# An attention loop whose SyncE transfers wait for earlier ones, so that 1.2 MB at most is under way

## The chip, the cores and the metric

The kernel runs on one core of a Trainium2 chip. The metric is the device time of one execution in microseconds. The times shown are those of three executions and of one that was profiled.

## The reference, cut to what matters

Attention over 8 batches of 8 heads (576 positions, 64 wide), four heads with a local mask and four with a strided one, then a mixture of 8 experts with one expert a token and a skip test.

```python
scores = scale * np.matmul(q, k.transpose(0, 1, 3, 2))
mask_local = (rel >= 0) & (rel < stride)
mask_strided = (rel >= 0) & (pos[None, :] % stride == pos[:, None] % stride)
scores = np.where(masks[None], scores, -1000000000.0)
attn = np.exp(scores - np.max(scores, axis=-1, keepdims=True))
attn = attn / (np.sum(attn, axis=-1, keepdims=True) + 1e-09)
x = np.matmul(attn, v)                 # then to 4608 tokens of 512
...
do_compute = x @ w_skip > 0
e_idx = np.argmax(xc @ w_gate, axis=1)
h = np.maximum(xc[mask] @ w1[e], 0.0)
y[mask] = gate_w[mask, None] * (h @ w2[e])
out[do_compute] = xc + y
```

## The kernel before

The attention works in 32 units: for each of 8 batches two units of the local heads (kind 0) and two of the strided ones (kind 1). The loop at the end of `attn_moe` runs over them. In its pass n TensorE (PE) multiplies queries and keys of unit n + 2 (`qk`, line 198), turns the scores of unit n (`tex`, line 233), multiplies with the values of unit n - 1 (`pv`, line 267) and turns the outcome of unit n - 2 (`xpose`, line 309). VectorE (DVE) adds masks and takes maxima (lines 205 to 211), divides (lines 275 to 282) and routes the tokens; GpSimd (POOL) subtracts the maxima (line 213); ScalarE (ACT) takes the exponential (line 241) and copies (line 311). The order on PE, DVE and POOL is written out by hand in the loop; that on ACT and SyncE is left to the planner, which keeps SyncE's transfers in the order of the program.

All plain transfers are issued by SyncE, one after the other:
- `loadq` and `loadk` (lines 172 and 177), one half of a batch's queries or keys in two transfers of 288 to 304 KB. They are issued in the odd passes, for the half batch n // 2 + 3.
- `loadv` (line 184), three transfers of 390 KB for kind 0 and two for kind 1, in the even passes, for the next batch.
- `store` (lines 290 and 295), the rows of a half batch that was done some units before: two transfers of 288 KB for kind 0, and six of 90 to 99 KB for kind 1.
- `wdma` (line 567), weights of the first expert, 512 KB each, five of them in the loop's last passes.

The tiles set how far loads run ahead: six for queries and keys together, two for the values of each kind, three for raw weights. A transfer that would write a tile waits until the last reader of the tile is done. Each transfer also counts up one of eight semaphores in turn when it lands, and the next one on that semaphore waits for it: so at most eight are under way, whatever their size.

Before the loop stand the loads of the first batch and half of the second. Behind it come the last stores, the routing of the last batch, and then the experts, whose tokens POOL gathers from the output by indirect DMA and whose weights SyncE loads two ahead of their use.

Of the kernel before, what the change touches and what calls it, by code (L numbers as in the profile page):

```python
# [2 lines left out]

# [19 lines left out]
NA = S // ST  # L23
HP = 64
# [14 lines left out]
QL = (S, S + PAD)  # L39
VL = (3, 2)  # L40
BIG = -(2.0 ** 33)
ESTR = 5120
COUNTED = {4: 3, 7: 5}
PB = 3
# [30 lines left out]
def make_consts():  # L75
# [8 lines left out]
    for t in range(5):  # L84
        ml[:, t] = np.where((i + 1 <= w) & (w <= i + ST) & (w >= (ST if t == 0 else 0)), 0.0, BIG)
    w = np.arange(SQ)[None, :]
    ms = np.where((i // NA == w // NA) & (w % NA <= i % NA) | (i >= SQ), 0.0, BIG)
    put("ml", ml.reshape(128, -1))
# [17 lines left out]
def attn_moe(ctx: ExitStack, tc: tile.TileContext, q, k, v, w9d, w1d, w2d, cst, out, NB=B):  # L106
    nc = tc.nc
# [5 lines left out]

    table = dpool.tile([NE * ESTR, 4], I32, name="table")

# [36 lines left out]
    frame = [ap.tile([128, 2, 6, HP], F32, name=f"frame{i}") for i in range(2)]  # L152

    qt_, kt_, vt_ = {}, {}, {}

    def part(d, L, kind, name):
        t = zp.tile([128, 2, S + PAD], F32, name=f"{name}{kind}", tag="qk", bufs=6)[:, :, 0:L[kind]]
# [11 lines left out]
    def loadq(b, kind):  # L169
        t, d = qtile(b, kind)  # L170
        for j in range(2):
            nc.sync.dma_start(t[:, j], d[:, j])

    def loadk(b, kind):
        t, d = ktile(b, kind)
        for j in range(2):
            nc.sync.dma_start(t[:, j], d[:, j])

    def loadv(b, kind):
        n, m = (LB, SP)[kind], VL[kind]  # L180
        vt_[b, kind] = vt = ap.tile([128, n, 4, 65], F32, name=f"vt{kind}", tag=f"vt{kind}", bufs=2)
        vr = vt.rearrange("p (t n) h c -> p t (n h c)", t=m)
        for t in range(m):
            nc.sync.dma_start(vr[:, t], v[b][kind * VL[0] + t])

# [96 lines left out]
    def store(b, kind):  # L284
        ob = out[b * S:(b + 1) * S, kind * 256:kind * 256 + 256]
        x = xt_[b, kind]
        for i in range(2):
            oc = ob[:, i * 128:(i + 1) * 128]
            if kind == 0:
                nc.sync.dma_start(oc.rearrange("(n q) c -> q n c", q=HP), x[HP * i:HP * i + HP])  # L290
            else:
                orr = oc.rearrange("(a r) c -> a r c", r=ST)
                for r in range(3):
                    m = (ST - r + 2) // 3
                    nc.sync.dma_start(orr[:, r::3, :], x[HP * i + r * NA:HP * i + (r + 1) * NA, 0:m, :])


    xT_ = {}
# [18 lines left out]
    def tiles(g):  # L317
        return GT
# [91 lines left out]
            counted(of)  # L410

    stores = []
    SYNC = mybir.DependencyInfo(mybir.DependencyClass.Sync, mybir.DependencyReason.DATA)

    def behind(i, them):
        for x in them:
            tc.add_manual_dep(i, x.name, SYNC, reason="the rows of a batch are stored before they are taken")
# [20 lines left out]
    def mul(g):  # L438
        o = slice(GOFF[g], GOFF[g + 1])
        lo, eh = hot_[g]  # L440
        pm = ap.tile([128, GT, NP, 24], BF16, name="hpm", tag="hpm", bufs=2)
        G.tensor_tensor(pm, eh.unsqueeze(2).broadcast_to([128, GT, NP, 24]),
                        parts[:, o, :].unsqueeze(3).broadcast_to([128, GT, NP, 24]), op=ALU.mult)
        hot_[g] = lo, pm
# [45 lines left out]
    def pick(b):  # L490
# [6 lines left out]
        V.tensor_reduce(fsel[:, 0:1], t1, axis=AX.X, op=ALU.add)  # L497
        V.tensor_scalar(fsel[:, 1:2], fsel[:, 0:1], float(ESTR), None, op0=ALU.mult)
        V.tensor_copy(isel[:, 0:2], fsel[:, 0:2])
# [15 lines left out]
    def sort(b):  # L515
# [10 lines left out]
        def places():  # L526
# [5 lines left out]
            V.tensor_reduce(orf[:, 0, :], big, axis=AX.X, op=ALU.add)  # L532
            V.tensor_scalar(orf[:, 1, :], orf[:, 0, :], float(ESTR), None, op0=ALU.mult)
            V.tensor_copy(order, orf)
# [28 lines left out]
    def wdma(key, e, j0, j1, after=()):  # L563
        for j in range(j0, j1):
            raw = early.tile([128, 1024], F32, name="raw", tag="raw", bufs=3)
            src = (w1d if j < 4 else w2d)[bass.ds(e, 1), j % 4]
            i = nc.sync.dma_start(raw, src.rearrange("o p c -> (o p) c")).ins
            for x in after:
                tc.add_manual_dep(i, x.name, SYNC, reason="the tokens come first")
            raw_[key, j] = raw  # L570
# [231 lines left out]
    p = ps("T")  # L802
# [10 lines left out]
    a, z = qtile(0, 0), ktile(0, 0)  # L813
# [27 lines left out]
    plan[CB + 1] = (None, 4 * CB + 11, None, None)  # L841
    pool_order = ExitStack()
    pool_order.enter_context(tc.manual_schedule(engines={G.engine, T.engine, V.engine}))
    for n, (b, pr) in enumerate(units):

        if pr % 2 == 0:
            if b + 1 < NB:
                loadv(b + 1, pr // 2)
            if n == 8:
                spare = tvw[:, CMAX:CE[0] * CE[1] + CT, :].rearrange("e (a n) c -> a e (n c)", n=NE)  # L850
                nc.sync.dma_start(spare, fill.rearrange("p n c -> p (n c)")[0:spare.shape[0]].unsqueeze(1)
                                  .broadcast_to([spare.shape[0], NE, 4 * NE]))
        else:
            if n > 4:
                store(units[n - 4][0], units[n - 4][1] // 2)
            g = n // 2 + 3
            if g // 2 < NB:
                loadq(g // 2, g % 2)
                loadk(g // 2, g % 2)
        if n + LA >= len(units) and "h" not in pool:  # L860
            zctx.close()
            pool["h"] = ctx.enter_context(tc.tile_pool(name="hpool", bufs=1, side="right", reuse_waits="tile"))
        g = [i for i, x in enumerate(GROUPS) if x[1] == b]

        front = [qk(*units[n + LA])] if n + LA < len(units) else []
        if n > 0:
            front.append(pv(*units[n - 1]))
        seq = [tex(b, pr)]
        if g and pr == 2:
            seq = [xpose(*units[n - 2])] + seq  # L870
        for x in front[:-1]:
            next(x)

        if len(front) > 1:
            run(seq.pop(0))
        if late:
            next(late[0])
        next(front[-1])
        put = [place(x) for x, it in plan.items() if it[3] == n]
        full = n == plan[CB][3]  # L880
        rank = []
        if ranked is not None:
            rank = [route2(ranked, of=COUNTED.get(b - 1))]
            for _ in range(tiles(ranked) + 1):
                next(rank[0])
            ranked = None

        if b > CB:
            run(*late)
            late = []  # L890
        for x in front:
            next(x, 0)
        run(*rank, *late, *front)
        if full:
            run(*put)
            tabled()
        late = []
        if b > 0 and pr == 2:
            seq = [score(b - 1, 0), score(b - 1, 1)] + seq
        if n > 1 and not (g and pr == 2):  # L900
            seq.append(xpose(*units[n - 2]))
        run(*seq)
        if not full:
            run(*put)
        if g and pr == 3:
            norm(g[0])
        if g and pr == 2:
            late = [route1(g[0])]
        if g and pr == 3:
            if b > CB:  # L910
                run(route2(g[0], of=COUNTED.get(b)))
            else:
                ranked = g[0]
        if b == PB + 2 and pr == 0:
            pick(PB)
        if (b, pr) in RESTS:
            j = RESTS.index((b, pr))
            wrest("e", j, j + 1)
        if (b, pr) in CASTS:
            j = CASTS.index((b, pr))  # L920
            wcast("e", j, j + 1)
        if b == CB + 2 and pr == 3:
            count(CB)
        if n == 1:
            G.tensor_copy(parts[:, :, 0:2], con["pk"].rearrange("p (t c) -> p t c", c=2))
        for x, it in plan.items():
            for f, at in zip((hot, gates, mul), (it[1], it[0], it[2])):
                if at == n:
                    f(x)
        if b == PB + 2 and pr == 3:  # L930
            e0 = nc.sync.value_load(isel[0:1, 0:1], min_val=0, max_val=NE - 1)
            wdma("e", e0, 0, 1)
        if b == PB + 2 and pr == 1:
            s0 = G.value_load(isel[0:1, 0:1], min_val=0, max_val=NE - 1)
        if (b, pr) in FETCH:
            j = FETCH.index((b, pr)) + 1
            wdma("e", e0, j, j + 1)
        if b == CB + 2 and pr == 1:
            rows("e", s0, *CE, eng=G)
            gather("e", "e", "e", last=(CB + 1) * S)  # L940
    pool_order.close()
    nr = len(GROUPS) - 1
    gates(CB + 1)
    mul(CB + 1)
    engines = ExitStack()
    engines.enter_context(tc.manual_schedule(engines={T.engine, A.engine, V.engine, G.engine}))
    run(pv(*units[-1]), xpose(*units[-2]), xturn("e"), xpose(*units[-1]))
# [7 lines left out]
    psum, bufs = pctx.enter_context(tc.tile_pool(name="psumT", bufs=1, space=PSUM, reuse_waits="tile")), {"S": 2, "T": 3, "PV": 2, "R": 1}  # L955
    s0n = G.value_load(isel[0:1, 2:3], min_val=0, max_val=(NE - 1) * ESTR + CE[0] * CE[1])
    ga = ffn1a("e")
# [201 lines left out]
```

## Time and profile before

| | us |
|---|---|
| three executions | 448.38, 450.92, 454.01 |
| their median | 450.92 |
| the profiled execution | 451.93 |
| its span, first to last instruction | 450.2 |
| PE busy | 412.2 |
| DVE busy | 280.2 |
| ACT busy | 186.6 |
| POOL busy | 142.6 |

The mean clock that was granted to PE in the profiled execution is 0.975 of full speed. Three executions lie within 5.6 us of each other, so that a single one says little about a difference of that size. SyncE moved 79.19 MB by its queue (q1 in the profile), POOL 10.37 MB by its own (q0), and 0.82 MB were instructions (q8 and q14).

In the rows of the profile an engine's name with a q is its sequencer: "SPq L172 ... x2" are two transfers issued at line 172. The time beside such a row is that of issuing, not of moving the bytes. "[1.30 <-X]" behind a row says that the engine stood idle for 1.30 us ahead of it and what ended that.

### The profile page before, as it was taken

The numbers are of one execution on the slowest core, as the hardware profiler recorded it, in microseconds if no ns is written. First come the engines' busy times: TensorE is split into PE (matmuls) and PEld (weight loads), VectorE is DVE, ScalarE is ACT, GpSimd is POOL, SyncE is SP. The second block draws the span as 40 slices with busy tenths as digits, with TensorE's granted clock in tenths as the row PEclk, the third lists the DMA queues.
The fourth block names the chain that finished last, engine by engine and source line by source line (L and its number), as shares of the span: only waits on it lengthen the run. The fifth ranks groups of instructions, "written<-read, shape, count | busy, mean of one in ns | idle before, by whom it ended". The sixth has DMA issues, their size and how long they took to land.

```text
span 450.2 us, 12195 instructions
## 1 busy us (share of the span) xinstructions
PE 412.2 (92%) x4991; PEld 370.6 (82%) x4992; DVE 280.2 (62%) x606; ACT 186.6 (41%) x370; POOL 142.6 (32%) x200
## 2 busy tenths in 40 slices
PE   6989898999789767999899999999999999999994
PEld 3766777777676655889799799999999999999984
DVE  4565695989997776781476464464474564755610
ACT  1334353536255416632533343444544535544400
POOL 3334444443555355024023318014024022200201
PEclk8899996999999889999999999999999999999998
DMA  8999987979995135515257476456566565645101
GB/s 296 397 393 322 369 283 270 296 239 321 309 378 164 34 101 154 179 62 146 86 162 229 131 226 209 140 166 206 163 200 184 161 210 181 218 150 183 48 20 42
DMA packets 51805, 90.38 MB, mean 201 GB/s; under 512 B 8251, under 2 KB 27963, under 8 KB 51745
## 3 DMA queue, kind: packets, MB, share of 16 engines
q1 hardware_dynamic: 45249, 79.19, 52.8%
q0 software_dynamic: 6496, 10.37, 8.0%
q8 instruction: 40, 0.66, 0.6%
q14 instruction: 20, 0.16, 0.1%
HBM read 75.16 MB, written 14.91 MB: 200 GB/s over the span
## 4 chain that ended last, share of the span: by engine, by line
PE 50%; DMA 1%; POOL 0%; DVE 0%; POOLq 0%; issue 0%
PE S L648 15%; PE S L650 15%; PE S L649 15%; PE PV L740 2%; PE T L642 1%; DMA xg<-out_dram,tab 1%; PE PV L782 0%; PE PV L780 0%; PE PV L781 0%; PE S L756 0%; PE S L755 0%; PE S L757 0%; POOL out_dram L728 0%; PE T L767 0%; PE S L642 0%; PE PV L642 0%
## 5 line engine op out<-in xcount | busy, mean ns | idle before, releaser
L648 PE MATMUL S<-xh,w1h 128*128 128x342 f32 (+6 forms) x248 | 78.6, 317 | 0.2 <-DVE hl L661 0.2
L650 PE MATMUL S<-xh,w1l 128*128 128x342 f32 (+6 forms) x248 | 76.7, 309 | 0.0
L649 PE MATMUL S<-xl,w1h 128*128 128x342 f32 (+6 forms) x248 | 76.5, 309 | 0.0
L728 POOL DMA_INDIRECT out_dram<-ot,tab x25 | 28.0, 1120 | 152.1 <-DVE ot L726 143.6
L648 PE MATMUL S<-hh,w2h 128*128 128x288 f32 (+5 forms) x192 | 59.5, 310 | 0.5 <-DVE hl L661 0.5
L650 PE MATMUL S<-hh,w2l 128*128 128x288 f32 (+5 forms) x192 | 58.0, 302 | 0.0
L649 PE MATMUL S<-hl,w2h 128*128 128x288 f32 (+5 forms) x192 | 57.9, 302 | 0.0
L660 ACT ACTIVATE hh<-S 128x342 fp32r<-128x342 f32 (+6 forms) x64 | 28.0, 437 | 63.4 <-PE S L650 58.3
L584 DVE TENSOR_TENSOR w1l<-raw,w1h 128x1024 fp32r<-128x1024 f32 x32 | 39.0, 1223 | 20.0 <-ACT w1h L578 20.0
L648 PEld LDWEIGHTS S<-xh,w1h 128*128 128x128 f32 x248 | 46.9, 189 | 0.9 <-issue 0.4
L649 PEld LDWEIGHTS S<-xl,w1h 128*128 128x128 f32 x248 | 46.8, 189 | 0.1
L213 POOL TENSOR_TENSOR sm<-sm,mx 128x480 f32<-128x480 f32 (+1 forms) x32 | 28.5, 910 | 57.7 <-DVE mx L211 36.7
L650 PEld LDWEIGHTS S<-xh,w1l 128*128 128x128 f32 x248 | 46.7, 188 | 0.0
L198 PE MATMUL S<-kt,qt 64*64 64x54 f32 (+1 forms) x1280 | 34.4, 244 | 13.4 <-issue 5.0
L584 DVE TENSOR_TENSOR w2l<-raw,w2h 128x1024 fp32r<-128x1024 f32 x32 | 39.1, 1223 | 9.8 <-ACT w2h L578 9.6
L198 PEld LDWEIGHTS S<-kt,qt 64*64 64x64 f32 x1280 | 28.1, 142 | 20.6 <-issue 8.5
L620 POOL DMA_INDIRECT xg<-out_dram,tab x25 | 33.9, 1357 | 33.9 <-issue 13.6
L661 DVE SCALAR_TENSOR_TENSOR hl<-S,hh 128x342 fp32r<-128x342 f32 (+6 forms) x64 | 30.9, 483 | 17.8 <-ACT hh L660 17.7
L311 ACT COPY xT<-T 128x512 f32<-128x512 f32 (+4 forms) x56 | 22.2, 441 | 36.8 <-PE T L309 36.6
L648 PEld LDWEIGHTS S<-hh,w2h 128*128 128x128 f32 x192 | 36.1, 188 | 0.8 <-DVE hl L661 0.8
L645 DVE TENSOR_TENSOR xl<-T,xh 128x288 fp32r<-128x288 f32 (+7 forms) x30 | 13.1, 468 | 37.3 <-ACT xh L644 37.3
L649 PEld LDWEIGHTS S<-hl,w2h 128*128 128x128 f32 x192 | 36.3, 189 | 0.0
(180 smaller groups left out, 828.2 us busy)
## 6 DMA issues: line engine op xcount, KB each, us to landing
raw<-in_w_dram SPq DMA_DIRECT2D x64, 512.0 KB
vt<-in_vp_dram SPq DMA_DIRECT2D x40, 390.0 KB
qt<-in_qp_dram SPq DMA_DIRECT2D x16, 304.0 KB
kt<-in_kp_dram SPq DMA_DIRECT2D x16, 297.0 KB
out_dram<-x SPq DMA_DIRECT2D x16, 288.0 KB
kt<-in_kp_dram SPq DMA_DIRECT2D x14, 304.0 KB
qt<-in_qp_dram SPq DMA_DIRECT2D x14, 288.0 KB
out_dram<-x SPq DMA_DIRECT2D x32, 99.0 KB
```

Source lines behind the costliest of these rows:

```text
L198: T.matmul(s[HP * (i ^ j):HP * (i ^ j) + HP, j, (blk - b0) * win:(blk - b0 + 1) * win], lhsT=qt[p, j, blk * nq:blk * nq + HP], rhs=kt[p, j ...
L213: G.tensor_tensor(e[:, j], e[:, j], mx[:, j].unsqueeze(2).broadcast_to([128, b1 - b0, win]), op=ALU.subtract)
L311: A.copy(xT_[b, kind][:, :, g * nq:(g + m) * nq].rearrange("p i (n q) -> p n i q", q=nq), t[:, 0:m * 128].rearrange("p (n i q) -> p n i q" ...
L584: V.tensor_tensor(lo, raw_.pop((key, j)), hi.bitcast(F32), op=ALU.subtract)
L620: i = G.indirect_dma_start(out=xg[:s["P"], t, :], out_offset=None, in_=out[0:last, :], in_offset=bass.IndirectOffsetOnAxis(ap=s["tab"][:s[ ...
L645: V.tensor_tensor(xl[:, c, :C], t[:, :C], xh[:, c, :C].bitcast(F32), op=ALU.subtract)
L648: T.matmul(p, lhsT=a[0], rhs=b[0], start=start, stop=False)
L649: T.matmul(p, lhsT=a[0], rhs=b[1], start=False, stop=False)
L650: T.matmul(p, lhsT=a[1], rhs=b[0], start=False, stop=stop)
L660: A.activation(s["hh"][:, f, :C], p[:, :C], AF.Relu)
L661: V.scalar_tensor_tensor(s["hl"][:, f, :C], p[:, :C], 0.0, s["hh"][:, f, :C].bitcast(F32), op0=ALU.max, op1=ALU.subtract)
L728: i = G.indirect_dma_start(out=out, in_=ot[:P], in_offset=None, bounds_check=NTOK - 1, oob_is_err=False, out_offset=bass.IndirectOffsetOnA ...
```

## The change

A helper `paced` issues a SyncE transfer and keeps it, with its size, in a list. While `steady` is set, from the loop's beginning to just behind its last pass, it goes back through the list from the newest, adding sizes to the new transfer's own. The first one with which the sum exceeds 1,200,000 bytes gets a dependency: the new transfer is issued only once that one has landed. The list also holds the transfers that were issued by the same functions ahead of the loop; those of the constants, the first unit's queries and keys, and a small fill aren't in it. All of `loadq`, `loadk`, `loadv`, `store` and `wdma` go through `paced`. Outside the loop it adds no dependency. Nothing is computed differently, and no transfer changes its place in the program.

```diff
+FLIGHT = 1200000
...
+    flight, steady = [], []
+
+    def paced(dst, src):
+        i = nc.sync.dma_start(dst, src).ins
+        size = 4 * math.prod(dst.shape)
+        left = FLIGHT - size
+        for x, n in reversed(flight if steady else []):
+            left -= n
+            if left < 0:
+                tc.add_manual_dep(i, x.name, SYNC, reason="few bytes are under way at a time")
+                break
+        flight.append((i, size))
+        return i
...
     def loadq(b, kind):
         t, d = qtile(b, kind)
         for j in range(2):
-            nc.sync.dma_start(t[:, j], d[:, j])
+            paced(t[:, j], d[:, j])
...
-            nc.sync.dma_start(vr[:, t], v[b][kind * VL[0] + t])
+            paced(vr[:, t], v[b][kind * VL[0] + t])
...
-                nc.sync.dma_start(oc.rearrange("(n q) c -> q n c", q=HP), x[HP * i:HP * i + HP])
+                paced(oc.rearrange("(n q) c -> q n c", q=HP), x[HP * i:HP * i + HP])
...
-            i = nc.sync.dma_start(raw, src.rearrange("o p c -> (o p) c")).ins
+            i = paced(raw, src.rearrange("o p c -> (o p) c"))
...
+    steady.append(True)
     for n, (b, pr) in enumerate(units):
...
     mul(CB + 1)
+    steady.clear()
```

More of the change, by code (lines that the diff above doesn't have):

```diff
@@ L1 @@
+import math
 from contextlib import ExitStack
@@ L154, in attn_moe @@
     qt_, kt_, vt_ = {}, {}, {}
+    flight, steady = [], []
+    SYNC = mybir.DependencyInfo(mybir.DependencyClass.Sync, mybir.DependencyReason.DATA)
+    def paced(dst, src):
[9 more added lines that the diff above has]
+        return i
     def part(d, L, kind, name):
@@ L176, in loadk @@
         for j in range(2):
-            nc.sync.dma_start(t[:, j], d[:, j])
+            paced(t[:, j], d[:, j])
     def loadv(b, kind):
@@ L294, in store @@
                     m = (ST - r + 2) // 3
-                    nc.sync.dma_start(orr[:, r::3, :], x[HP * i + r * NA:HP * i + (r + 1) * NA, 0:m, :])
+                    paced(orr[:, r::3, :], x[HP * i + r * NA:HP * i + (r + 1) * NA, 0:m, :])
     xT_ = {}
@@ L412, in attn_moe @@
     stores = []
-    SYNC = mybir.DependencyInfo(mybir.DependencyClass.Sync, mybir.DependencyReason.DATA)
     def behind(i, them):
```

## The prediction

> **What bounds the kernel now.** I read the page first (totals, then the slices), then the stages by windows, then who waits for whom on TensorE, and only then single stretches of the timelines.
>
> ```profile
> span 450.2 us, 12195 instructions
> PE 412.2 (92%) x4991; PEld 370.6 (82%) x4992; DVE 280.2 (62%) x606; ACT 186.6 (41%) x370; POOL 142.6 (32%) x200
> ...
> DMA  8999987979995135515257476456566565645101
> GB/s 296 397 393 322 369 283 270 296 239 321 309 378 164 34 101 154 179 62 146 86 162 229 131 226 209 140 166 206 163 200 184 161 210 181 218 150 183 48 20 42
> ...
> 14.30:70.00 55.70, 47.28 (x1099) 37.89 (x1099) 39.28 (x97) 23.19 (x55) 20.41 (x32) 0.99 1.00 351
> 70.00:140.00 70.00, 63.81 (x1411) 51.94 (x1412) 59.58 (x166) 32.12 (x76) 33.85 (x65) 0.96 0.89 300
> 140.00:180.00 40.00, 29.96 (x553) 23.87 (x550) 29.43 (x96) 17.29 (x42) 19.93 (x32) 0.91 0.32 90
> 211.00:450.20 239.20, 231.33 (x1570) 222.83 (x1568) 127.00 (x184) 98.57 (x169) 54.73 (x45) 1.00 0.51 159
> ```
>
> In the slices (11.3 us each) the DMA engines are 70 to 90% busy and more for the first 13 and half busy behind. The last four lines are stretches of the windows view: length, then busy time (and count) of PE, PEld, DVE, ACT and POOL, granted clock, DMA share, GB/s. From 211 us on the experts keep PE busy for 97% of the time; nothing of the change reaches in there. The attention loop runs from 14 to about 180 us. In its first 126 us the DMA engines are 89 to 100% busy, and PE is idle for 55.7 - 47.3 = 8.4 us and 70 - 63.8 = 6.2 us. DVE is busy for 71% of the first stretch and 85% of the second. So PE sets the first, and in the second DVE is close behind. What ended PE's idle time is the next question, first up to 215 us, then (last line) from 215 us on:
>
> ```profile
> PE S L198 <- issue: 5.0, 4, 2.3
> PE PV L267 <- issue: 3.0, 3, 1.3
> PE T L233 <- issue: 2.1, 7, 0.3
> PE S L198 <- DMA kt<-in_kp_dram: 1.7, 4, 0.6
> PE T L399 <- issue: 1.3, 1, 1.3
> ...
> PE S L642 <- DMA xg<-out_dram,tab: 1.5, 2, 0.9
> ```
>
> "issue" means that the profile shows nothing that PE waited for, yet it stood in the middle of a run of equal matmuls. Behind the loop there is none of it: the last line is all that the view has there. On PE's timeline these stops look like this (idle before the row in brackets), with the DMA view of 0.1 us from 28.0 and 0.2 us from 67.0:
>
> ```profile
> 24.23 0.27 PE L233 MATMUL T<-cs,frame 128*54 128x128 f32 x1 [0.35 <-issue]
> 27.08 0.91 PE L198 MATMUL S<-kt,qt 64*64 64x54 f32 x44 [0.46 <-DMA kt<-in_kp_dram]
> 30.64 0.69 PE L267 MATMUL PV<-vt,pts 54*64 54x65 f32 x25 [1.03 <-issue]
> 36.84 0.89 PE L198 MATMUL S<-kt,qt 64*64 64x96 f32 x27 [0.64 <-issue]
> 50.27 0.91 PE L267 MATMUL PV<-vt,pts 54*64 54x65 f32 x39 [1.30 <-issue]
> 55.60 0.56 PE L267 MATMUL PV<-vt,ptl 96*64 96x65 f32 x11 [0.71 <-issue]
> 66.34 0.90 PE L198 MATMUL S<-kt,qt 64*64 64x54 f32 x42
> 69.52 0.47 PE L198 MATMUL S<-kt,qt 64*64 64x54 f32 x6 [2.28 <-issue]
> 91.14 0.68 PE L198 MATMUL S<-kt,qt 64*64 64x54 f32 x29 [1.43 <-issue]
> 132.67 0.23 PE L399 MATMUL T<-rohb,oneb 128*128 128x24 bf16 x3 [1.26 <-issue]
> 138.93 0.49 PE L198 MATMUL S<-kt,qt 64*64 64x96 f32 x13 [0.64 <-issue]
> ...
> q8 instruction: 1, 0.02, 69.9%
> ...
> q8 instruction: 1, 0.02, 33.1%
> ```
>
> Queue 8 carries instructions, 16 KB at a time. One such packet starts at 28.0 to 28.1 and PE goes on at 30.64; one starts at 67.0 to 67.2 and PE goes on at 69.52, 42 matmuls into a group of 48. So **PE runs out of instructions**, and goes on about 2.5 us after the packet with the next block starts. The packet itself holds one of 16 DMA engines for about 0.699 x 0.1 x 16 = 1.1 us. It starts late because of what is ahead of it. Two stretches from one such packet to the next, in the loop and among the experts:
>
> ```profile
> 56.93:67.08 10.15, 9.86 (x236) 7.54 (x234) 9.39 (x20) 5.58 (x14) 4.97 (x5) 1.00 0.86 273
> 287.38:305.37 17.99, 17.99 (x128) 17.94 (x127) 10.80 (x15) 8.41 (x14) 2.84 (x3) 1.00 0.52 159
> ```
>
> Among the experts a packet comes after 128 + 127 = 255 PE instructions; in the loop 470 passed before one came. How deep the queue ahead of it is, SyncE shows (the first line is a wait of SyncE's, the others its issues):
>
> ```profile
> SPq L184 <- DMA vt<-in_vp_dram: 2.8, 6, 0.6
> ...
> 18.04 1.02 SPq L172 DMA_DIRECT2D qt<-in_qp_dram  x2
> 19.71 1.31 SPq L177 DMA_DIRECT2D kt<-in_kp_dram  x2
> ...
> 67.47 1.54 SPq L177 DMA_DIRECT2D kt<-in_kp_dram  x2
> 73.82 0.85 SPq L184 DMA_DIRECT2D vt<-in_vp_dram  x2
> ...
> 128.26 1.77 SPq L177 DMA_DIRECT2D kt<-in_kp_dram  x2
> ...
> 150.95 0.79 PE L198 MATMUL S<-kt,qt 64*64 64x54 f32 x18 [1.01 <-DVE sm L205]
> ```
>
> The keys issued by 19.71 + 1.31 = 21.02 let PE go on at 27.08: 6.1 us from issue to use, at 350 to 390 GB/s some 2.1 to 2.4 MB ahead of and in that transfer. That is 7 or 8 transfers of 300 to 400 KB.
>
> **The change, part by part.** (1) The wait itself: each q, k, v load, each store and each expert-weight load that SyncE issues in the loop now waits until enough earlier ones have landed that it and those still under way are at most 1.2 MB: three loads of q and k or of v, two of weights, more of the small stores. The queue ahead of an instruction packet falls from about 2.3 to at most 1.2 MB, so by up to 1.1 MB at 351 GB/s = 3.1 us. The longest stop is 2.28 us, so all nine of them could go: 5.0 + 3.0 + 1.3 + 0.35 = 9.65 us. If the cut were half of that (1.55 us), 0.73 us of the longest would stay. I leave 1.0 us, 0.6 of it before 70 us and 0.4 behind.
> How much of it is on the path: before 70 us the stops are 0.35 + 1.03 + 0.64 + 1.30 + 0.71 + 2.28 = 6.3 us; 5.7 of these go, and I count 85% (PE's busy share there) = 4.9 us. Behind 70 us they are 1.43 + 1.26 + 0.64 = 3.3 us; 2.9 of these go, and with DVE at 85% I count 60% = 1.7 us. Sum 6.6 us; the bounds are 0 (the queue isn't the reason) and 9.6.
>
> (2) What is late next: the loads. The new wait is on SyncE, and behind it stand the next loads, the stores, and late in the loop the expert number and the weights. PE waits for loads where they are used soon after their issue, which is at 26.3 to 27.1 us (the kt row above), and never for those of the second half: the keys issued at 128.26 are used at 150.95. With a bound, the stream runs at full rate only if three loads take longer to move than one takes from issue to landing. Three of 304 KB are 0.93 MB, at 351 GB/s 2.65 us. What one takes alone:
>
> ```profile
> 198.68 0.33 SPq L567 DMA_DIRECT2D raw<-in_w_dram  x1
> ...
> GB/s 0 0 0 0 0 0 0 0 0 0 246 123 246 164 164 246 164 451 328 410 369 410 492 287 451 451 123 82 41 0 0 0 0 27 31 4 0 0 0 0
> ...
> DMA packets 28058, 40.57 MB, mean 323 GB/s; under 512 B 2212, under 2 KB 15878, under 8 KB 28032
> ...
> q8 instruction: 20, 0.33, 1.0%
> ```
>
> The slices are 0.1 us each from 198.6 on: issued at 198.68, a 512 KB load with nothing ahead of it has its first bytes at 199.6 and its last at 201.4, so 2.7 us, 0.9 of it before the first byte. A 304 KB load with others ahead keeps the 0.9 and needs 0.89 for its own bytes; the landing notice that comes on top is not in these rows, between 0 and 1 us. That is 1.8 to 2.8 us beside 2.65: the rate falls by 0 to 6%. On top, each instruction packet holds one engine for 1.1 us, and with three loads under way the next issue waits for that engine: the last rows (14.3 to 140 us) have 20 of them, so up to 22 us over the stretch; the deep queue of now has other bytes for the other engines meanwhile. Against this stand 11% of the second stretch in which the DMA engines are idle (7.7 us), and the 23 us between issue and use of the last keys. At 26 to 27 us there is no such cushion: the four q and k loads ahead of that use are among the first that the bound delays. I take 1.0 us later there (bounds 0 and 2, as one packet's 1.1 us falls into it or not, or two do) and nothing elsewhere.
>
> (3) No cost elsewhere: the stores come later by a few us, and who waits for them, the gathers behind the loop and a reuse of the x tiles eight units on, stands far behind. The weights' loads of the loop are bounded too; ACT and DVE cast them long after. From the loop's end on, nothing is bounded. SyncE's additional waits are on no other engine's path as long as the loads are in time; if that cover goes, it is the third rival.
>
> Sum: - 6.6 + 1.0 = -5.6 us. The profiled run took 451.93 us (1.7 beside its span), so it would take 446.3; it lies 1.0 us above the median of the three runs, 450.92, and against that I predict **445.4 us**.
>
> [...]
>
> **The rivals.** *Nothing is gained.* The packet is late for another reason than the bytes ahead of it: it goes on a queue of its own, and if a DMA engine took turns between queues, it would wait for one packet of SyncE's, whatever stands behind. For it: the 1.1 us that a packet takes is the same at 28 us in a full queue and at 67. Against it: 470 instructions between packets in the full queue and 255 in the half-empty one. Time: the sum without its first term, 450.9 + 0 to 1 = 451.4. [...]
>
> *Slower: the loads become the bound.* The place is PE's wait for qt and kt. The loop needs 40.57 MB between 14.3 and 140 us, and the last keys by 151: 40.57 / 136.7 = 297 GB/s decides. With three loads under way the rate is 0.93 to 1.2 MB over the time from issue to landing, so below 297 from 3.1 us (q, k) to 4.0 us (v) on; about 3.6 for the mix. At 4.0 us it is about 265 GB/s: 153 us instead of 126, so ready at 167 less the few us of stores at its end, some 10 us later than now used: 460 us. For it: a 1.1 us instruction packet now and then, on top of 1.8 to 2.8 us. Against it: 2.7 us for 512 KB alone, and the 23 us ahead.
>
> *More is gained.* All nine stops go and all of it counts, nothing is late: 450.9 - 9.65 = 441.3, and a load that PE waits for less (1.7 us in all) would make it 440.
>
> **How the numbers follow.** The forecast (stops mostly gone, loads in time) 0.60, around 445.4, by itself 442 to 449; nothing gained 0.21, 449 to 453; loads as the bound 0.11, 454 to 470; more gained 0.08, 438 to 442. The range of 8 in 10 leaves out the half of the last that lies lowest and most of the loads' case: 440.5 to 454. Two per cent (9 us), about what a measurement of this kernel can tell from no change, is 441.9 on one side and 459.9 on the other. Faster by more: the last case and a tail of the first, 0.14; slower by more: 0.07, as half of the loads' case is dearer than 9 us; within: 0.79.
>
> **What would show it.** Right: PE's waits up to 215 us have "issue" near 2 us rather than 11; instruction packets start about every 256 PE instructions; SyncE's waits name DMA far oftener; the DMA share between 14 and 140 us falls a little, and the loads end later than 140. Wrong: the "issue" rows stay; or "PE S L198 <- DMA kt" and "qt" grow from 1.7 us to several, which is the slower rival; or PE's idle time moves to "DVE" by as much as "issue" loses.

## The result, and the profile after

Slower: 474.96 us, the median of four executions (472.56 to 476.16), beside 449.83 us for the kernel before (four executions, 448.38 to 454.01). The ratio is 1.054, with a 95% interval of 1.045 to 1.062. The profiled execution took 476.16 us, its span is 474.5. The helper stands above the code, so the lines have moved by 14 or 16: `qk` is now line 214, `tex` 249, `pv` 283, and every bounded transfer shows the helper's line 161.

The totals and the slices of the page, the same stretches of the windows view as before, and the DMA view of 14.3 to 140 us:

```profile
span 474.5 us, 12223 instructions
PE 424.1 (89%) x4991; PEld 380.4 (80%) x4992; DVE 281.5 (59%) x606; ACT 187.2 (39%) x370; POOL 142.3 (30%) x200
...
PEclk9789898799898967899999999999999999999998
DMA  8988886888787787542434736746656566545201
GB/s 293 329 256 240 240 261 197 248 250 233 227 256 230 228 243 212 162 136 92 122 99 163 233 112 208 233 139 181 192 176 195 170 184 206 193 158 179 84 20 40
...
14.30:70.00 55.70, 47.89 (x1003) 38.81 (x1001) 35.31 (x84) 22.58 (x52) 18.98 (x32) 0.92 0.85 259
70.00:140.00 70.00, 57.53 (x1170) 46.06 (x1170) 51.28 (x141) 25.84 (x63) 27.18 (x50) 0.90 0.79 235
140.00:180.00 40.00, 29.36 (x607) 24.01 (x606) 27.02 (x74) 15.93 (x36) 15.32 (x26) 0.84 0.80 236
235.00:474.50 239.50, 231.60 (x1571) 223.03 (x1569) 127.05 (x184) 98.79 (x170) 54.57 (x45) 0.99 0.51 159
...
DMA packets 21480, 30.89 MB, mean 246 GB/s; under 512 B 1728, under 2 KB 12081, under 8 KB 21457
```

In the first stretch 259 GB/s are moved where it was 351, in the second 235 where it was 300: from 14.3 to 140 us 30.89 MB instead of 40.57. The stream that used to be over at about 140 us now runs until 180. The last row has the experts: 231.6 us of PE as before (231.3), so the whole 24 us are in the attention loop. TensorE's waits up to 240 us, then its row in the page's costliest groups, then SyncE's waits from 14 to 200 us:

```profile
PE S L214 <- DMA kt<-in_kp_dram: 20.1, 18, 3.1
...
PE T L249 <- issue: 1.7, 6, 0.3
PE PV L283 <- issue: 0.4, 1, 0.4
...
L214 PE MATMUL S<-kt,qt 64*64 64x54 f32 (+1 forms) x1280 | 39.0, 260 | 30.6 <-DMA kt<-in_kp_dram 20.1
...
SPq L161 <- DMA qt<-in_qp_dram: 25.5, 25, 2.9
SPq L161 <- DMA vt<-in_vp_dram: 25.2, 24, 2.5
SPq L161 <- DMA kt<-in_kp_dram: 22.5, 25, 2.9
SPq L161 <- DMA out_dram<-x: 11.1, 15, 1.5
```

The stops without a named cause ("issue") went from 11.4 us in fifteen (9.65 of it in the nine long ones) to 2.1 us in seven of at most 0.4. In their place TensorE waits 18 times, for up to 3.1 us, for keys: 20.1 us instead of 1.7. Of these, 4.2 us lie ahead of 14 us (0.6 before the change); their loads are issued ahead of the loop, where nothing is bounded, and in the profiles of this document that part differs from 0.4 to 4.2 us. SyncE waits 84 us for landings (25.5 + 25.2 + 22.5 + 11.1) instead of 13, which is the bound at work. That the keys end the loop shows at its end, on SyncE's and on PE's timeline:

```profile
166.89 2.30 SPq L161 DMA_DIRECT2D qt<-in_qp_dram  x2
170.36 1.13 SPq L161 DMA_DIRECT2D kt<-in_kp_dram  x2
...
174.22 0.46 PE L214 MATMUL S<-kt,qt 64*64 64x54 f32 x4 [3.49 <-DVE acc L472]
174.97 1.53 PE L214 MATMUL S<-kt,qt 64*64 64x54 f32 x44 [0.29 <-DMA kt<-in_kp_dram]
...
199.42 1.57 PE L283 MATMUL PV<-vt,pts 54*64 54x65 f32 x40
```

Before, the keys of that unit were used at 150.95, 15 us after they had landed; now they land at 174.8 (by the semaphore's events in the trace) and are used at 174.97. The row at 174.22 names DVE, but the first half of the same keys had landed at 174.09, so these 3.5 us are probably a wait for keys too. The loop's last matmuls with the values end at 201.0 instead of 177.0 us.

### The profile page after: what moved, and what is told of

The parts are those of the page before. It is cut to its first block, busy times and chain, and to the rows that moved or that the text cites. A ratio compares the mean times of both kernels' runs of the same rounds, so it can differ in the third digit from the quotient of the medians.

```text
span 474.5 us, 12223 instructions
## 1 busy us (share of the span) xinstructions
PE 424.1 (89%) x4991; PEld 380.4 (80%) x4992; DVE 281.5 (59%) x606; ACT 187.2 (39%) x370; POOL 142.3 (30%) x200
## 5 line engine op out<-in xcount | busy, mean ns | idle before, releaser
L214 PE MATMUL S<-kt,qt 64*64 64x54 f32 (+1 forms) x1280 | 39.0, 260 | 30.6 <-DMA kt<-in_kp_dram 20.1
L214 PEld LDWEIGHTS S<-kt,qt 64*64 64x64 f32 x1280 | 32.1, 156 | 38.7 <-issue 18.3
L634 POOL DMA_INDIRECT xg<-out_dram,tab x25 | 33.7, 1348 | 34.2 <-issue 10.4
L257 ACT ACTIVATE ptl<-T 96x512 f32<-96x512 f32 (+1 forms) x40 | 20.2, 547 | 47.1 <-PE T L249 47.1
```

The costliest lines, as they stand in the source:

```text
L214: T.matmul(s[HP * (i ^ j):HP * (i ^ j) + HP, j, (blk - b0) * win:(blk - b0 + 1) * win], lhsT=qt[p, j, blk * nq:blk * nq + HP], rhs=kt[p, j ...
L257: A.activation(pt[:w, (g + x) * 128:(g + y) * 128], t[:w, x * 128:y * 128], AF.Exp, scale=0.125)
L634: i = G.indirect_dma_start(out=xg[:s["P"], t, :], out_offset=None, in_=out[0:last, :], in_offset=bass.IndirectOffsetOnAxis(ap=s["tab"][:s[ ...
```

## The experiments

The kernels differ from the one after by their FLIGHT, or as their diffs show. Times from issue to landing are taken from each SyncE instruction's start to the last event of its semaphore. Theory A: three transfers under way are too few to cover the time from issue to landing. Theory B: each wait costs by itself, whatever the bound.

**The size of the bound.**

```diff
-FLIGHT = 1200000
+FLIGHT = 600000      # bound_06; 1600000 bound_16; 2000000 bound_20
```

> The bound is 0.6 MB, so one load of 300 to 400 KB is under way at a time, and small stores several. Theory A: every load takes its whole time from issue to landing, 2.7 to 3.2 us with nothing beside it; some 100 loads, 16 large stores and 7 groups of small ones between 14 us and the end of the loop take 330 to 380 us, so the run takes 600 to 660 us, with no issue stops. Theory B: the waits are as many as at 1.2 MB, so the time grows far less, to under 520 us.

> The bound is 1.6 MB in place of 1.2 MB: five loads of q and k or four of v under way. Theory A (too few transfers are under way for the 3.8 us that a load takes from issue to landing at 1.2 MB): five in 3.8 us is 0.76 us a load, the full rate again, so TensorE waits for kt and qt for under 3 us in all instead of 20; the queue is still 0.8 MB shorter than the 2.4 MB without the bound, so the issue stops stay under 3 us; 443 to 449 us. Theory B (each wait for a landing costs something by itself, whatever the bound): as many waits as at 1.2 MB, so TensorE's wait for kt stays above 12 us and the time above 465 us.

> The bound is 2.0 MB: six loads of q and k, five of v. Theory A: loads at full rate, kt and qt waits under 3 us; the queue is only 0.4 MB shorter than without a bound (1.1 us at 351 GB/s), so of the 9.65 us of issue stops 2 to 5 us stay; 445 to 451 us. Theory B: above 460 us.

Measured: 623.46 us with 0.6 MB (one execution; before 448.63); 451.31 with 1.6 MB, ratio 1.002 (0.998 to 1.007); 444.22 with 2.0 MB, ratio **0.987 (0.979 to 0.995): faster than both kernels**, though whether by 2% is open. TensorE's wait for kt up to 235 us (161.3 us up to the loop's end) and the two stretches with 0.6 MB, its wait for kt with 1.6 MB, and its waits and the two stretches with 2.0 MB:

```profile
PE S L214 <- DMA kt<-in_kp_dram: 108.1, 21, 13.3
14.30:70.00 55.70, 31.93 (x654) 25.89 (x652) 20.41 (x45) 14.03 (x32) 11.02 (x15) 0.79 0.45 138
70.00:140.00 70.00, 32.75 (x605) 27.02 (x605) 24.29 (x69) 13.07 (x31) 14.16 (x29) 0.68 0.45 121
```

```profile
PE S L214 <- DMA kt<-in_kp_dram: 7.8, 10, 1.9
```

```profile
PE S L214 <- DMA kt<-in_kp_dram: 6.6, 7, 1.8
PE T L249 <- issue: 1.4, 5, 0.3
PE T L415 <- issue: 0.5, 1, 0.5
PE S L214 <- issue: 0.5, 1, 0.5
14.30:70.00 55.70, 50.87 (x1168) 41.23 (x1166) 40.31 (x100) 25.41 (x61) 21.27 (x33) 0.96 0.96 324
70.00:140.00 70.00, 65.37 (x1493) 52.24 (x1494) 62.82 (x172) 35.11 (x83) 37.08 (x68) 1.00 0.96 311
```

The bound's size decides, not the waits: B falls. With 2.0 MB the stops are as short as with 1.2 MB (2.4 us) and the rate is almost that of before. A was right in kind, and with 0.6 MB in size too. It was too hopeful for 1.6 MB: TensorE still waited 7.8 us for kt there (3.9 of it ahead of 14 us) and had 5.3 us of stops, both above A's 3 us, and the time was above A's 443 to 449. With 2.0 MB its wait for kt was 6.6 us (3.5 of it ahead of 14 us), also above A's 3, and the time just below A's 445 to 451.

**Only a part of the loop.**

```diff
-    steady.append(True)
     for n, (b, pr) in enumerate(units):
+        if n == 12:
+            steady.append(True)
```

> The bound of 1.2 MB holds from pass 12 of 32 on, as the loads have run ahead by then; before that there is none. Theory A: the rate of 240 to 250 GB/s is below the 297 that the loop needs, so the lead of 8 to 13 us is used up within two to three batches and TensorE waits for kt again for 5 to 10 us in all; 455 to 464 us. Rival C (only the first third is hurt, since loads have no lead there; later a lead of 13 us covers the slower rate): no waits for kt, and the issue stops after pass 12 (5 to 6 us) are gone: 444 to 448 us.

```diff
     steady.append(True)
     for n, (b, pr) in enumerate(units):
+        if n == 12:
+            steady.clear()
```

> The bound of 1.2 MB for the first 12 passes alone; from there on nothing is bounded. Theory A (lateness of the loads adds up; the loop ends later by what the last keys are late beyond the 15 us that they lay ready before): with the bound throughout the last keys were 39 us late, with the bound from pass 12 on 16.5; so the first 12 passes make them about 22 late, of which at full rate afterwards some is made up since the tiles are then free earlier than the loads need: 10 to 22 late, the loop ends 2 to 8 us later than before, 452 to 459 in all, with TensorE's waits for kt 8 to 14 us and nearly all of them before 100 us. Theory B' (only the waits count, wherever they lie: 24 us over 32 passes): 12 of 32 passes cost 9 us, 459.

Measured: 455.67 us from pass 12 on (1.015, 1.008 to 1.023), 458.38 up to pass 12 (1.020, 1.012 to 1.028; before 448.95). TensorE's wait for kt, first from pass 12 on, then up to pass 12:

```profile
PE S L214 <- DMA kt<-in_kp_dram: 6.5, 8, 1.8
```

```profile
PE S L214 <- DMA kt<-in_kp_dram: 12.6, 11, 3.4
```

Theory A holds in both, but for the loop's end up to pass 12, which is 8.3 us later instead of 2 to 8; rival C falls. Up to pass 12 the 459 of B' fits as well; it is the pair that decides. Twenty of the 32 passes cost 7 us, the first twelve 9: a wait has no price of its own, or the twenty would have cost the more. With the bound up to pass 12 TensorE waited for kt 12.6 us, though the last keys then landed 36 us ahead of the loop's end: in the first third the loads have no lead, and lateness is paid at once. Later most of it is covered by the 15 us of lead: in the profile from pass 12 on the last keys land 16.5 us later than before and the loop ends 1.3 us later. That execution was 2.8 us faster than the median of its kernel, so the size is rough.

**The last landing and the loop's end** put all runs into one table (us; the landing and the end are those of the profiled executions, whose time is the last column):

| bound | last keys land | last `pv` ends | between | median time | profiled time |
|---|---|---|---|---|---|
| none (before) | 135.8 | 177.0 | 41.2 | 449.83 | 451.93 |
| 2.6 MB | 131.1 | 171.9 | 40.8 | 448.15 | 446.13 |
| 2.0 MB | 139.3 | 170.1 | 30.8 | 444.22 | 444.55 |
| 2.0 MB from pass 6 | 137.1 | 169.6 | 32.5 | 443.86 | 445.24 |
| 1.2 MB up to pass 12 | 149.1 | 185.3 | 36.2 | 458.38 | 459.82 |
| 1.6 MB | 150.0 | 176.2 | 26.2 | 451.31 | 452.56 |
| 1.2 MB from pass 12 | 152.3 | 178.3 | 26.0 | 455.67 | 452.86 |
| 1.2 MB, loads only | 161.9 | 187.2 | 25.3 | 464.12 | 463.64 |
| 1.2 MB (after) | 174.8 | 201.0 | 26.2 | 474.96 | 476.16 |
| 0.6 MB | 321.1 | 346.8 | 25.7 | 623.46 | 623.46 |

In the last five rows the loop ends 25 to 26 us behind the last landing, whatever the bound: the loads set its end. (With 1.6 MB it is a tie: the last keys land 0.2 us ahead of their use, and the stop there is put down to DVE.) Where more lies between, TensorE and DVE set it, with what they lost to keys earlier, as up to pass 12, whose last keys land no later than with 1.6 MB.

**Do the stores belong to the bound?**

```diff
-                paced(oc.rearrange("(n q) c -> q n c", q=HP), x[HP * i:HP * i + HP])
+                nc.sync.dma_start(oc.rearrange("(n q) c -> q n c", q=HP), x[HP * i:HP * i + HP])
```

> The bound of 1.2 MB for the loads alone; the stores neither wait nor count. They are 21% of the loop's bytes. Theory A (the time from issue to landing is mostly fixed, 3.8 us with three under way, and the stores find room beside the loads): the loads keep 245 GB/s for themselves, the stores come on top, some 300 GB/s in all from 14 to 140 us; the last keys land at 145 to 155 us, as with a bound of 1.6 MB, and the time is 449 to 457. Rival D2 (the engines in this loop move about 245 GB/s of whatever mix when only three loads are under way, so that stores lengthen the loads' time to 4.5 us and more): the last keys land at 165 to 175 us and the time stays at 465 to 476.

Measured: 464.12 us, 1.035 (1.029 to 1.041), the last keys at 161.9: between the two, and neither is borne out; D2, with its 465 to 476, is the nearer. The rate from 14.3 to 140 us is 265 GB/s instead of 246, and the loads take longer to land (q 4.6, k 3.7 and v 4.5 us on average instead of 3.8, 3.8 and 4.15). Stores beside the loads are worth some rate, as other bytes under way are, and take some of the loads' own.

**The transfers by themselves.**

```diff
+COUNTS = ((1, 10), (2, 20), (3, 24), (4, 24), (5, 24), (6, 24), (8, 24))
+MIXES = ((1200000, (0, 1, 2)), (2000000, (3, 4, 5)), (None, (6, 7)))
...
+    for count, n in COUNTS:
+        for m in range(n):
+            half(q[at // 2 % B], QL, 1, at % 2, count=count if m >= count else None, alone=m == 0 and at > 0)
...
+                loadv(b, kind, **kw)
+                store(b, kind, **kw)
...
+                    half(q[b], QL, kind, j, **kw)
...
+                    half(k[b], KL, kind, j, **kw)
```

> All computation is left out; only transfers remain. Seven groups of loads of 304 KB, with 1, 2, 3, 4, 5, 6 and 8 under way at a time, then three stretches with the loop's own mix of loads and stores (values, stores, queries and keys of a batch in turn), bounded to 1.2 MB, to 2.0 MB and by nothing but the eight semaphores. Theory A (a fixed part of each transfer's time, of about 1.9 us, has to be covered by the bytes of others): one alone takes 2.8 us from issue to landing as it did in the loop with one under way; three take 2.8 to 3.0 us each, since 3 x 304 KB are then only 2.65 us of moving, so 310 to 330 GB/s; from four on the engines are full, about 390 GB/s, and the time grows by 0.8 us with each further load: 3.2, 4.0, 4.8 and 6.4 us for 4, 5, 6 and 8. The mix at 1.2 MB then reaches 300 GB/s and the loop's 245 has to be put down to what runs beside it. Rival D (already the loads among themselves get in each other's way, whatever else runs): three take 3.6 to 4.0 us, 235 to 255 GB/s, and the mix at 1.2 MB gives 235 to 255 GB/s, as in the loop.

The planner had moved stores between the loads of the first two groups, so these and the mix can't be read. The groups of 3 to 8 are clean: 274, 301, 349, 395 and 411 GB/s. Three under way take 3.4 us each: A (310 to 330 GB/s) and D (235 to 255) both miss, and the engines are full from six on, not from four. One kernel more keeps the order of the program, and has twelve loads instead of ten in its first group:

```diff
+    order.enter_context(tc.manual_schedule(engines={nc.sync.engine}))
```

> As loads_alone, all computation left out, but with the transfers in the program's order: in loads_alone the stores of the mix had come forward between the loads of the first two groups, and the mix at 1.2 MB was measured with stores missing. Theory E (a packet costs more at an engine whose queue had run empty, so the moving of the bytes itself gets slower when few bytes wait): the groups of 3, 4, 5, 6 and 8 repeat 274, 301, 349, 395 and 411 GB/s within 3%, one alone takes 2.7 to 3.0 us (100 to 115 GB/s), two 3.1 to 3.3 us (190 to 200); the mean time of a packet of 2432 bytes falls from over 135 ns with two to 98 ns with eight under way. The mix, with its smaller packets, reaches 235 to 260 GB/s at 1.2 MB, 280 to 310 at 2.0 MB and 310 to 340 with eight, so that the loop's 246, 317 and 323 are those of the transfers by themselves. Rival F (what runs beside the loop takes a tenth of the rate): the mix at 1.2 MB reaches 265 GB/s or more.

Its numbers, by the trace's landings and packets:

| under way | issue to landing, us | GB/s | mean packet of 2432 bytes, ns |
|---|---|---|---|
| 1 | 2.76 | 112 | 137 |
| 2 | 3.12 | 198 | 142 |
| 3 | 3.40 | 274 | 127 |
| 4 | 4.05 | 309 | 118 |
| 5 | 4.48 | 348 | 111 |
| 6 | 4.73 | 405 | 104 |
| 8 | 6.11 | 410 | 102 |
| mix, 1.2 MB | 3.76 (q, k), 4.14 (v) | 253 | |
| mix, 2.0 MB | 4.38, 5.01 | 322 | |
| mix, eight | 5.27, 6.60 | 323 | |

The mix at 1.2 MB, with nothing beside it, lands in 3.76 and 4.14 us; in the loop it was 3.83 and 4.15. So the loop's rate is, to 3%, that of the transfers themselves (246 GB/s in the loop, 253 here), and F falls; E holds, but for 2.0 MB, which is better than it said (322 instead of 280 to 310). D's second figure, 235 to 255 GB/s for the mix at 1.2 MB, comes true here as well; A's 300 doesn't. What the rate is lost to, the DMA view shows for the mix at 1.2 MB (194.9 to 256.5 us) and with eight (314 to 347.7):

```profile
DMA packets 12131, 15.56 MB, mean 253 GB/s; under 512 B 834, under 2 KB 7522, under 8 KB 12130
...
q1 hardware_dynamic: 12130, 15.55, 83.7%
```

```profile
DMA packets 8402, 10.88 MB, mean 323 GB/s; under 512 B 582, under 2 KB 5190, under 8 KB 8401
...
q1 hardware_dynamic: 8401, 10.88, 93.5%
```

The share of 16 engines over the packets is the time of one: 0.837 x 16 x 61.6 us / 12130 = 68 ns against 0.935 x 16 x 33.7 / 8401 = 60 ns. Of the 22% that the rate is lower, about half are engines without work (0.837 / 0.935 = 0.90) and half slower packets (60 / 68 = 0.88). In the kernels it is the same. Their rows for 14.3 to 140 us, before and after, give 0.924 x 16 x 125.7 / 28032 = 66 ns and 0.805 x 16 x 125.7 / 21457 = 75 ns:

```profile
q1 hardware_dynamic: 28032, 40.20, 92.4%
```

```profile
q1 hardware_dynamic: 21457, 30.55, 80.5%
```

Slower is not every packet, but a share of them. By the trace's packets of 2432 bytes the median is 98 ns in every group of the table, and also in the kernels before and after, whose means are 106 and 125 ns. Behind the first landings of a group (as many as it has under way), 14% of the packets take over 150 ns with one load, 9% with three and none with eight. With one load alone nearly all of the slow ones (209 of 210) lie in the first half of their load, so they go with the start of moving and not with its course.

**The bound without its effect, and a later start.**

```diff
-FLIGHT = 1200000
+FLIGHT = 2600000      # bound_26
```

> 2.6 MB, about as much as eight transfers hold. Theory (the stops without a named cause come from the bytes ahead of an instruction packet, and the bound costs nothing where it doesn't bind): TensorE's stops without a named cause in the loop are back to 7 to 11 us, TensorE waits for kt 1 to 3 us, the rate from 14 to 70 us is 340 to 355 GB/s, and the time is 447 to 452, no different from before. Rival (the stops went because SyncE's issues are spread by the waits, not because fewer bytes are queued): the stops stay below 5 us and the time below 446.

Measured: 448.15 us, 0.999 (0.995 to 1.003). The helper costs nothing where it seldom binds, and the gain of 2.0 MB is gone. In the profile, that of the fastest of ten executions, the stops are 6.0 us, less than the 7 to 11 expected, and the wait for kt 6.2, more than the 1 to 3 (4.1 of it ahead of 14 us). The rate from 14 to 70 us is 347 GB/s, as expected:

```profile
PE S L214 <- DMA kt<-in_kp_dram: 6.2, 6, 2.0
PE S L214 <- issue: 2.6, 3, 1.4
PE T L249 <- issue: 1.4, 5, 0.3
PE T L415 <- issue: 1.3, 1, 1.3
PE PV L283 <- issue: 0.7, 1, 0.7
```

The rival (stops below 5 us, time below 446) fails on both.

```diff
-    steady.append(True)
     for n, (b, pr) in enumerate(units):
+        if n == 6:
+            steady.append(True)     # and FLIGHT = 2000000
```

> 2.0 MB, and only from pass 6 on. With 2.0 MB from the start TensorE still waited 3.0 us for kt at 26 to 29 us, where the loads are used soon after their issue; before the change it waited 0.8 us there. Theory A: these waits fall to the 1 us of before, and of the stops without a named cause those of the first six passes come back (2.0 us); about as fast as 2.0 MB throughout, 442 to 446, faster than before by 1 to 1.5%. If the early waits for kt are worth more than the stops, 441 to 443; if less, 444 to 446.

Measured: 443.86 us, 0.988 (0.983 to 0.992).

```profile
PE S L214 <- DMA kt<-in_kp_dram: 3.0, 5, 1.5
PE T L249 <- issue: 1.8, 6, 0.3
PE T L415 <- issue: 1.7, 1, 1.7
PE PV L283 <- issue: 1.0, 1, 1.0
```

TensorE waits 3.0 us for kt instead of 6.6, and at 26 to 27 us 0.75 us, as before the change (0.76) and as expected. Of the stops of the first six passes that of 1.0 us is back, at 30.6 us; that of 1.7 us lies at 125 us, where the bound of 2.0 MB holds. The time can't be told from that with 2.0 MB throughout.

## Why the prediction was wrong

It said 445.4 us and 440.5 to 454; it was 474.96, and the rival "the loads become the bound", with a chance of 0.11, is what happened, at a higher price than its 454 to 470. (Two small slips change nothing: 450.92 - 5.6 is 445.3, and the DMA engines are over 70% busy in the first 12 slices, not 13.)

*Step 1 was right in kind.* The stops went, 11.4 us to 2.1, as the prediction's first sign asked ("near 2 us rather than 11"). The second sign, a packet about every 256 PE instructions (255 among the experts before), came only in part: between 14 and 160 us they are 128 to 365 apart, and were 107 to 485. What that is worth shows where the loads still keep up: with 2.0 MB the time is 4.4 us lower than the 448.63 of the same chip. The prediction counted 6.6. Between 14.3 and 180 us TensorE's stops are 8.9 us shorter there than before, while its waits for DVE grow by 3.7 us and those for keys by 2.0. In one profile each, the stops are 11.4 us before, 6.0 with 2.6 MB, 2.4 with 2.0 (4.5 from pass 6 on), 5.3 with 1.6, 2.1 with 1.2 and 1.1 with 0.6: fewer with a smaller bound, but not in every step. Part of the differences is scatter: with 2.6 MB as many bytes are under way as before (2.0 MB on average at an issue between 14.3 and 140 us in both; 1.7 with the bound of 2.0), and yet the stops are 5.4 us apart. That the bytes ahead make the packet late is therefore borne out by the direction and by the gain with 2.0 MB; no trace shows when a packet was asked for. The rival "nothing is gained" falls by that gain; its condition, that a DMA engine takes turns between queues, no run shows.

*Step 2 failed*, in this sentence: "That is 1.8 to 2.8 us beside 2.65: the rate falls by 0 to 6%." The time of one load was right: one alone takes 2.76 us, the upper end of that. (The landing notice, for which it allowed 0 to 1 us, came 0.29 us behind the last packet of the 512 KB load that it quotes, at 201.92 and 201.63 us in the trace of before.) But it was taken for a load's time with two others under way, and that is 3.40 us for equal loads (311,296 bytes each, 274 GB/s) and 3.8 to 4.15 in the loop's mix. The rate fell by 24% (323 to 246 GB/s). Two things were left out. The time from issue to landing grows with each load under way: 2.76, 3.12 and 3.40 us for one, two and three. And more of the packets are slow when few bytes are queued, so that their mean is 127 ns with three loads and 102 with eight, and the engines are 80% busy at 246 GB/s. The instruction packets that the prediction feared instead are not it: the mix alone, with one of them in 61.6 us, moves 253 GB/s. The one price that the step set, 1.0 us (0 to 2) for the keys used at 26 to 27 us, came out at 2.7: TensorE waits 3.05 + 0.42 us for them instead of 0.30 + 0.46.

*The cushion was counted too long.* Its "23 us between issue and use of the last keys" holds their way to landing too; what lay ready was 15 us. The last keys came 39 us later, so 24 were left, and that is the loss.

*The rival's arithmetic was right, its rate too high.* It set the limit at 297 GB/s, reached by 3.1 us (q, k) or 4.0 (v); measured are 3.8 and 4.15, both over. Its 460 us came from 265 GB/s. With 246 the same sum is 40.57 / 0.246 = 165 us, so ready at 179 less the few us of stores: 174.8 it was. The evidence against it that was quoted, 512 KB in 2.7 us with nothing ahead, says nothing of three at once, and so 0.11 was too little.

*Step 3 was right:* behind the loop nothing changed (273.5 us of span after the last `pv`, 273.2 before).

## What to carry to other kernels

How many bytes a queue needs for its full rate is read with several transfers under way: the time of one alone (2.76 us here) is no measure of three (3.40 us each). Whether the bytes count or the number of transfers is not shown, since nearly all loads here have 288 to 390 KB. Here 1.2 MB gives three quarters of the rate and 2.0 MB nearly all of it, while 2.0 MB already makes the stops shorter (2.4 and 4.5 us in two profiles, 11.4 before). A lead of loads is counted from landing to use (15 us here, where issue to use is 23), and here it paid for a lower rate only once it had been built up: with the bound in the first twelve passes alone TensorE waited 12.6 us for kt, with it from there on 6.5.

## What was not expected of the hardware

The DMA engines' busy share hid a part of the fall in the rate: in the first stretch it went from 1.00 to 0.85 while the rate went from 351 to 259 GB/s, since more of the packets were slow, and the share is made of their times. Of that stretch's packets of 2432 bytes, whose median is 98 ns in both traces, those over three times the median are 1.1% before and 4.9% after, and the mean went from 107 to 124 ns.

TensorE's granted clock was lower in the kernels in which it waited more. From 14.3 us to about the loop's end, before and after:

```profile
14.30:176.90 162.60, 138.97 (x3041) 111.98 (x3040) 125.26 (x343) 70.63 (x167) 71.98 (x123) 0.96 0.80 272
```

```profile
14.30:200.80 186.50, 151.76 (x3049) 122.71 (x3047) 127.39 (x346) 72.26 (x168) 72.36 (x123) 0.88 0.80 237
```

The same matmuls took 151.8 us instead of 139.0, at a mean granted clock of 0.88 instead of 0.96. TensorE was busy for 85% of that stretch before and 81% after; with 0.6 MB for 57% and 47% of the two stretches shown, at 0.79 and 0.68. Within one kernel it doesn't hold for every stretch (before: 0.99 while 85% busy, 0.96 while 91%), and what lowers the clock no run shows. The clock isn't what set the time: SyncE, which issues the loads, waits 84 us for landings and 6 us for TensorE, and from the first use of the last keys to the end of the last `pv` it is 201.0 - 175.0 = 26.0 us, as before with 177.0 - 151.0.
